# Sinkhorn attention and a four-expert layer: one score stage two slots forward, one weight load in two parts

## The chip, the cores and the metric

The kernel runs on one core of one Trainium2 chip. The metric is the device time of one execution in microseconds (us). Before the change it is 362.58 us (median of three runs, 362.51 to 362.75). The profile covers one further execution of 362.67 us, whose instructions span 360.9 us.

The engines carry the profile's names: PE is the matrix engine (TensorE), PEld its weight loads, DVE is VectorE, ACT is ScalarE, POOL is GpSimd, SP is SyncE. L414 is line 414 of the kernel before.

## The reference, cut to what matters

An attention over four batches of eight heads with 768 tokens, whose keys and values are mixed among eight blocks by a doubly normalized matrix, feeds a layer of four experts.

```python
def _attn_ref(q, k, v, sort_net):            # q, k, v: (4, 8, 768, 64), sort_net: (4, 8, 8, 8)
    P = sort_net
    for _ in range(5):                       # exp, rows to sum 1, columns to sum 1
        ...
    k_sorted = np.einsum('bhij,bhjcd->bhicd', P, k_b).reshape(B, H, S, D)
    v_sorted = np.einsum('bhij,bhjcd->bhicd', P, v_b).reshape(B, H, S, D)
    ...
    scores = scale * np.matmul(q_b, k_sb.transpose(0, 1, 2, 4, 3))   # within a block of 96 tokens
    attn = np.exp(scores - max) ; attn = attn / (sum + 1e-9)
    return np.matmul(attn, v_sb)

def _moe_ref(x, domain_probs, w1, w2):       # x: (3072, 512), w1: (4, 512, 1024), w2: (4, 1024, 512)
    p = domain_probs / (domain_probs.sum(-1, keepdims=True) + 1e-09)
    for e in range(E):
        h = np.maximum(x @ w1[e], 0.0)
        out += p[:, e:e + 1] * (h @ w2[e])
```

## The kernel before, where the change touches it

The instruction order of every engine is the order of the program text. The experts' layers of one batch run on PE while the attention of a later batch is done in small stages between them. A stage handles one pair of heads. These are the stages that matter here; `psa` hands out the tiles of one PSUM pool, `psm` those of another, and each pool has two buffers that are taken in turn.

```python
    psM = ... tc.tile_pool(name="psM", bufs=2, space=PSUM)     # hidden layers and outputs of the experts
    psA = ... tc.tile_pool(name="psA", bufs=2, space=PSUM)     # attention stages

    def st_k(b, pr):                  # mixed keys of a pair: 6 matmuls, four copies by ACT
        ps = psa([P, 2, 512], F32, f"ps_k_{b}_{pr}")
        ...
        kT = kTs[pr % 2][...]
        ... nc.scalar.copy(kT[...], pk[...])                   # line 404

    def st_s(b, pr):                  # scores of a pair: both buffers, 16 matmuls, two exponentials by ACT
        kT, qT = kTs[pr % 2], qTs[(b, pr)]
        pss = [psa([P, 2, 512], F32, f"ps_s_{b}_{pr}_{hh}") for hh in range(2)]
        for i in range(NB):
            for hh in range(2):
                nc.tensor.matmul(pss[hh][...], kT[...], qT[...], start=True, stop=True)   # line 414
        for hh in range(2):
            nc.scalar.activation(ETs[2 * (pr % 2) + hh][...], pss[hh][...], AF.Exp, ...)  # line 421

    def normalize(ps, xsl, hh):       # DVE
        ...
        nc.vector.reciprocal(rz[:], av[:, :, :, D:D + 1])                                 # line 430
        nc.vector.tensor_tensor(xsl[...], av[:, :, :, 0:D], rz[:].broadcast_to(...), ALU.mult)

    def st_a(b, pr):                  # output of a pair: a buffer for each head, normalized by DVE
        ...
        for hh in range(2):
            ps = psa([P, 2, 512], F32, f"ps_a_{b}_{pr}_{hh}")
            for i in range(NB):
                nc.tensor.matmul(ps[...], ET[...], vs[...], start=True, stop=True)        # line 449
            normalize(ps, xsl, hh)

    # st_v(b, pr): mixed values (2 matmuls, a copy by ACT, line 361);  st_q: transposes queries by a transfer
```

The hidden layers of the experts are computed in groups. After each group a slot is called, in which the stages planned for that slot are put into the program. `Hb` and `Sb` hold a hidden layer and its sums.

```python
    def chunk_first(b, c, es, first, slot, weights=None):
        for e in es:
            for g in range(2):
                ps = psm([P, 4, 2 * P], F32, f"ps_h_{b}_{c}_{e}_{g}")
                ... nc.tensor.matmul(ps[:, f, :], w1sb[e][...], xT[...], ...)   # 16 of them, line 780
                nc.vector.scalar_tensor_tensor(out=Hb[...], in0=ps[:], ...)     # line 786
                ... h_sums(e - 1, w)                                            # DVE, lines 750 and 752, after g = 1
                slot()

    PLANS = {   # (chunk, slot, stage, batch, pair)
        1: [
            (0, 0, st_k, 2, 1), (0, 0, st_bk, 2, 1), (0, 1, st_lk, 3, 0), (0, 1, st_n, 3, 1), (0, 2, st_q, 2, 3), (0, 3, st_a, 2, 0),
            (0, 3, st_n, 3, 2), (0, 4, st_s, 2, 1), (0, 5, st_x, 2, 0), (0, 5, st_k, 2, 2), (0, 5, st_v, 2, 2),
            ... (0, 6, st_v, 2, 3), ... (0, 7, st_s, 2, 2), ...
```

The second matrix of expert 0 is loaded by one transfer from POOL's queue. PE uses it in `second_layer0`, four of its eight parts first, then a slot, then the other four.

```python
    def load_w2(e):
        nc.gpsimd.dma_start(w2sb[e][:], moe_w2[e].rearrange("(fc p) d -> p fc d", p=P))

    def second_layer0(hf, slot):
        for t in range(R // 2):
            ...
            for fc in range(NFC):                                               # NFC is 8
                nc.tensor.matmul(ps, h0(fc)[...], w2sb[0][:, fc, :], ...)       # line 704
                if fc == KH - 1:                                                # KH is 4
                    slot()
            if col == 0:
                own_weights(po[:, 1, 0:R])
            ...
            slot()

    load_half_queries(1)
    load_w2(0)
    build_PI0(nc.gpsimd, 1, 0, H, Rs[:, 0:H, HB:NB])                            # POOL, line 323
```

Of the kernel before, what the change touches and what calls it, by code (L numbers as in the profile page):

```python
# [17 lines left out]
def kernel(  # L18
# [11 lines left out]
    nc = tc.nc  # L30
# [8 lines left out]
    P = 128  # L39
# [5 lines left out]
    NFC = FF // P  # L45
# [80 lines left out]
    w1sb, w2sb = [], []  # L126
# [8 lines left out]
                w1sb[e][:, ds(i * n, n)], moe_w1[e].rearrange("(kc p) f -> p kc f", p=P)[:, ds(i * n, n)]  # L135
            )

    def load_w2(e):
        nc.gpsimd.dma_start(w2sb[e][:], moe_w2[e].rearrange("(fc p) d -> p fc d", p=P))

    def load_half_queries(hf):
        for qd in range(2):
            nc.gpsimd.dma_start(
                q0[ds(64 * qd, 64), hf].rearrange("p h r d -> p h (r d)"), half_queries(qd, hf)
            )
# [176 lines left out]
    def build_PI0(eng, a, h0, hn, src):  # L322
        eng.tensor_tensor(
            PI0[a][:, ds(h0, hn)],
            maskk[:, 0:HB * CP].rearrange("p (o i c) -> p o i c", o=1, c=CP).broadcast_to([P, hn, HB, CP]),
            src.rearrange("p g (i o) -> p g i o", o=1).broadcast_to([P, hn, HB, CP]),
            ALU.mult,
        )
# [280 lines left out]
    def st_bk(b, qd):  # L609
# [16 lines left out]
            (2, 9, st_k, 2, 0), (2, 9, st_lv, 3, 0), (2, 9, st_n, 3, 0), (2, 11, st_s, 2, 0), (2, 12, st_q, 2, 2),  # L626
        ],
        1: [
            (0, 0, st_k, 2, 1), (0, 0, st_bk, 2, 1), (0, 1, st_lk, 3, 0), (0, 1, st_n, 3, 1), (0, 2, st_q, 2, 3), (0, 3, st_a, 2, 0),
            (0, 3, st_n, 3, 2), (0, 4, st_s, 2, 1), (0, 5, st_x, 2, 0), (0, 5, st_k, 2, 2), (0, 5, st_v, 2, 2),  # L630
            (0, 5, st_n, 3, 3), (0, 6, st_v, 2, 3), (0, 6, st_lv, 3, 1), (0, 7, st_s, 2, 2), (0, 8, st_k, 2, 3),
            (0, 8, st_bv, 3, 0), (0, 9, st_bk, 3, 0), (0, 9, st_lk, 3, 1), (0, 9, st_q, 3, 0), (0, 10, st_a, 2, 1),
            (0, 11, st_s, 2, 3), (0, 12, st_a, 2, 2), (0, 12, st_x, 2, 1), (0, 12, st_q, 3, 1), (0, 13, st_v, 3, 0),
# [691 lines left out]
    mixed("k", 0, mk0, 2, 2, act)  # L1325
    vec(Rs.rearrange("p g (a i) -> p a g i", a=2), Rv.rearrange("p a i g -> p a g i"))
    load_half_queries(1)
    load_w2(0)
    build_PI0(nc.gpsimd, 1, 0, H, Rs[:, 0:H, HB:NB])
    h_w(0, vec, 0, 2, tails[("v", 0, 0)])  # L1330
    mixed("v", 0, mv0, 2, 2, vec)
# [50 lines left out]
    def builds(b):  # L1382
        for n in range(2 * b, 2 * b + 2):
            build_PI(nc.gpsimd, n, "v")
            build_PI(nc.gpsimd, n, "k")

    load_w2(1)
    load_w2(2)
    load_w1(3)
    load_w2(3)  # L1390
# [99 lines left out]
```

The softmax here doesn't subtract the row's maximum and nothing guards it: scores larger than these inputs give would overflow.

## Time and profile before

| what | before |
|---|---|
| time, median of 3 | 362.58 us |
| span of the profiled execution | 360.9 us |
| PE busy | 352.6 us |
| PE's wait in the score stage of line 414 for DVE | 1.3 us, in 2 waits |
| PE's wait at line 704 for the load of a second matrix | 0.4 us, 1 wait |

In the profile, busy time is the time in which an engine ran instructions; an engine's wait is its idle time just before an instruction, put down to whatever released that instruction last. In a list in order of time the columns are start, duration, engine, line, operation, what is written and read, and the number of instructions drawn together; idle time and its releaser follow in brackets. `ps_s` is the score tile, `ps_a` the output tile of the attention, `ps_h` a hidden layer, `xsl` the normalized output, `w` a weight matrix.

### The profile page before, as it was taken

To read this page: it belongs to the slowest core of one execution; us is meant where nothing else is said; L and a number is where in the kernel's file an instruction comes from. 1 tells how busy PE (TensorE), PEld (TensorE's weight loads), DVE (VectorE), ACT (ScalarE), POOL (GpSimd) and SP (SyncE) were. 2 spreads that over 40 slices of the span, in tenths; PEclk is the share of its full clock that TensorE was granted. 3 is DMA by queue.
4 is the path that set the end of the run, shared out by engine and by line. 5 is a ranking of instruction groups with operands and counts; after the bars stand their busy time and mean duration, and the time that the engine had idled before them with its cause. 6 is when DMAs were issued, how large, how long until landed. Compare 5 with 4: busy or idle time off the path is not lost.

```text
span 360.9 us, 9496 instructions
## 1 busy us (share of the span) xinstructions
PE 352.6 (98%) x3949; PEld 306.6 (85%) x3949; DVE 275.2 (76%) x549; ACT 172.4 (48%) x306; POOL 133.2 (37%) x148
## 2 busy tenths in 40 slices
PE   8899999999999989999999999999999999999995
PEld 8785857888888968988889888888888888888895
DVE  5753897769798677868988988896678886588962
ACT  2664440442425254367947348831289611688210
POOL 8882010367022420000534518840058800288400
PEclk9999999999999999999999999999999999999999
DMA  7999999999999999935995330004300016100011
GB/s 100 207 206 231 213 210 198 210 180 189 190 178 158 192 107 158 180 69 69 176 187 101 54 124 0 2 0 107 101 30 2 3 39 137 61 0 2 2 73 46
DMA packets 72007, 40.52 MB, mean 112 GB/s; under 512 B 40598, under 2 KB 66716, under 8 KB 71964
## 3 DMA queue, kind: packets, MB, share of 16 engines
q0 software_dynamic: 36560, 19.93, 42.6%
q1 hardware_dynamic: 35260, 19.92, 28.1%
q8 instruction: 31, 0.51, 0.6%
q14 instruction: 12, 0.10, 0.1%
q10 hardware_dynamic: 144, 0.07, 0.1%
HBM read 42.13 MB, written 6.34 MB: 134 GB/s over the span
## 4 chain that ended last, share of the span: by engine, by line
PE 87%; DMA 5%; DVE 4%; issue 1%; ACT 1%; POOL 1%; DVEq 0%; ACTq 0%
PE ps_h L780 17%; PE ps_Q L1234 16%; PE ps_p L764 12%; PE ps_X L1104 10%; PE ps_Z L1104 6%; PE ps_Q L1104 6%; PE ps_Z L1234 6%; DMA w<-in_moe_w_dram 4%; PE ps_o L704 3%; PE ps_p L815 3%; PE ps_s L414 2%; PE ps_h L669 1%; PE ps_a L449 1%; PE ps_v L361 1%; PE ps_k L395 1%
## 5 line engine op out<-in xcount | busy, mean ns | idle before, releaser
L780 PE MATMUL ps_h<-xT,w 128*128 128x256 f16 x576 | 67.5, 273 | 0.0
L780 PEld LDWEIGHTS <-w 128*128 128x128 f16 x576 | 55.2, 98 | 7.3
L786 DVE SCALAR_TENSOR_TENSOR Hb<-ps_h,pb 128x1024 f16<-128x1024 f32 x34 | 41.5, 1223 | 18.3 <-PE ps_h L780 17.9
L1104 PEld LDWEIGHTS <-w 128*128 128x128 f16 x480 | 43.5, 98 | 4.9 <-issue 0.2
L1117 POOL TENSOR_TENSOR arena<-tmp,pb 128x512 f16<-128x512 f32 x12 | 15.2, 1276 | 65.1 <-PE ps_Z L1104 49.8
L1234 PEld LDWEIGHTS <-Hb 128*128 128x128 f16 x320 | 31.1, 98 | 3.6
L421 ACT ACTIVATE ET<-ps_s 96x768 f16<-96x768 f32 x24 | 18.0, 802 | 30.8 <-PE ps_s L414 30.6
L1234 PEld LDWEIGHTS <-Sb 128*128 128x128 f16 x304 | 28.0, 98 | 3.4 <-DVE Sb L750 0.3
L1116 ACT ACTIVATE tmp<-tmp 128x512 f32<-128x512 f32 x46 | 28.9, 632 | 4.2 <-DVE tmp L1154 4.2
L1104 PEld LDWEIGHTS <-arena 128*128 128x128 f16 x312 | 27.8, 98 | 2.8
L404 ACT CAST kT<-ps_k 64x384 f16<-64x384 f32 x48 | 22.7, 473 | 14.0 <-PE ps_k L395 13.0
L121 POOL DMA_DIRECT2D arena<-in_q_dram x24 | 19.9, 843 | 18.2 <-DMA q_ring<-arena 17.1
L1104 PE MATMUL ps_X<-ET,arena 128*128 128x256 f16 x168 | 25.2, 272 | 0.0
L764 PEld LDWEIGHTS <-Hb 128*128 128x128 f16 x232 | 21.9, 98 | 3.0
L1234 PE MATMUL ps_Q<-w,Hb 128*128 128x256 f16 x192 | 24.4, 273 | 0.0
L1110 DVE SCALAR_TENSOR_TENSOR Hb<-ps_X,pb 128x512 f16<-128x512 f32 x27 | 18.6, 691 | 7.4 <-PE ps_X L1104 7.3
L1124 ACT COPY ps_X<-ps_Z 128x512 f32<-128x512 f32 x27 | 15.4, 570 | 18.1 <-PE ps_Z L1104 18.1
L1104 PE MATMUL ps_Z<-xT,w 128*128 128x256 f16 (+1 forms) x176 | 22.5, 258 | 0.1
L750 DVE TENSOR_TENSOR Sb<-Hb 128x512 f16<-128x512 f16 x33 | 21.2, 661 | 0.0
L1131 ACT COPY tmp<-ps_X 128x512 f32<-128x512 f32 x26 | 15.2, 585 | 8.8 <-PE ps_X L1104 6.2
L1110 DVE SCALAR_TENSOR_TENSOR Hb<-ps_Z,pb 128x512 f16<-128x512 f32 x27 | 18.4, 682 | 1.3 <-PE ps_Z L1104 1.3
L1154 DVE TENSOR_TENSOR tmp<-ps_Q,tmp 128x512 f32<-128x512 f32 x26 | 17.7, 681 | 0.8 <-PE ps_Q L1104 0.8
(261 smaller groups left out, 742.4 us busy)
## 6 DMA issues: line engine op xcount, KB each, us to landing
w<-in_moe_w_dram POOLq DMA_DIRECT2D x7, 1024.0 KB, 27.7
pb<-p_dram SPq DMA_DIRECT2D x9, 512.0 KB, 6.1
arena<-in_k_dram POOLq DMA_DIRECT2D x8, 384.0 KB, 8.6
arena<-in_v_dram POOLq DMA_DIRECT2D x8, 384.0 KB, 7.7
vs<-arena SPq DMA_DIRECT2D x36, 66.0 KB, 5.1
arena<-in_q_dram POOLq DMA_DIRECT2D x24, 96.0 KB, 7.3
out_dram<-ob SPq DMA_DIRECT2D x9, 256.0 KB, 2.1
out_dram<-oa SPq DMA_DIRECT2D x8, 256.0 KB, 2.4
```

Source lines behind the costliest of these rows:

```text
L121: nc.gpsimd.dma_start(t[:, h // 2, :, h % 2, :], q[b, h].rearrange("(t p) d -> p t d", p=P))
L404: nc.scalar.copy(kT[ds(D * hh, D), r], pk[ds(D * r, D), hh].rearrange("p a (i c) -> p a i c", c=CP),)
L421: nc.scalar.activation(ETs[2 * (pr % 2) + hh][:, 0:S].rearrange("c (a x) -> c a x", a=2), pss[hh][0:BLK, :, 0:HS], AF.Exp, bias=0.0, scale ...
L750: tt(sm[0], blk(0, 1), blk(1, 1), ALU.add)
L764: nc.tensor.matmul(ps, lhs(e, f), Ts[e][rhs][:, f, :], start=(first and e == es[0] and f == 0), stop=(done and e == es[-1] and f == KH - 1 ...
L780: nc.tensor.matmul(ps[:, f, :], w1sb[e][:, kc, ds((4 * g + f) * P, P)], xT[:, kc, ds(2 * c * P, 2 * P)], start=(kc == 0), stop=(kc == NKC ...
L786: nc.vector.scalar_tensor_tensor(out=Hb[:, homes.get(e, e), ds(4 * g, 4), :], in0=ps[:], scalar=0.0, op0=ALU.max, in1=weights(e).broadcast ...
L1104: nc.tensor.matmul(dst[:, ds(f * cols, cols)], a[lhs][:, k, ds((f0 + f) * P, P)], t[rhs][:, k, :], start=(first and f == 0 and k == 0), st ...
L1110: nc.vector.scalar_tensor_tensor(out=home(i, j), in0=src.rearrange("p (f x) -> p f x", f=m), scalar=0.0, op0=ALU.max, in1=weight(j).broadc ...
L1116: nc.scalar.activation(src, src, AF.Relu, bias=0.0, scale=1.0)
L1154: tt(t12, Q, u2, ALU.add)
L1234: nc.tensor.matmul(ps, lhs(e, f), Ts[e][rhs][:, f, part], start=(first and e == 0 and f == 0), stop=(e == E - 1 and f == KH - 1), skip_gro ...
```

## The change

In the plan for batch 1, the score stage of batch 2's second pair moves from slot 4 to slot 2 of the first chunk. It then stands ahead of `st_a` of the first pair, in slot 3, where it stood behind it. It is meant to keep the scores from having to wait until DVE has emptied the two buffers that `st_a` fills. The second matrix of expert 0 is loaded in two halves of four parts each, so that the first matmuls that use it depend on the first half alone.

```diff
-    def load_w2(e):
-        nc.gpsimd.dma_start(w2sb[e][:], moe_w2[e].rearrange("(fc p) d -> p fc d", p=P))
+    def load_w2(e, parts=1):
+        n = NFC // parts
+        for i in range(parts):
+            nc.gpsimd.dma_start(
+                w2sb[e][:, ds(i * n, n)], moe_w2[e].rearrange("(fc p) d -> p fc d", p=P)[:, ds(i * n, n)]
+            )
@@ PLANS @@
-            (0, 0, st_k, 2, 1), (0, 0, st_bk, 2, 1), (0, 1, st_lk, 3, 0), (0, 1, st_n, 3, 1), (0, 2, st_q, 2, 3), (0, 3, st_a, 2, 0),
-            (0, 3, st_n, 3, 2), (0, 4, st_s, 2, 1), (0, 5, st_x, 2, 0), (0, 5, st_k, 2, 2), (0, 5, st_v, 2, 2),
+            (0, 0, st_k, 2, 1), (0, 0, st_bk, 2, 1), (0, 1, st_lk, 3, 0), (0, 1, st_n, 3, 1), (0, 2, st_q, 2, 3), (0, 2, st_s, 2, 1), (0, 3, st_a, 2, 0),
+            (0, 3, st_n, 3, 2), (0, 5, st_x, 2, 0), (0, 5, st_k, 2, 2), (0, 5, st_v, 2, 2),
@@ program @@
-    load_w2(0)
+    load_w2(0, 2)
```

## The prediction

> **What bounds the kernel now.** I read the page's shares first, then who waits for whom on TensorE, then the order of time around each of its waits.
>
> ```profile
> PE 352.6 (98%) x3949; PEld 306.6 (85%) x3949; DVE 275.2 (76%) x549; ACT 172.4 (48%) x306; POOL 133.2 (37%) x148
> ```
>
> TensorE (PE) is busy 98% of the span, so only time in which it stands still can be won by moving work about. The second view is the list of waits on PE, longest total first (columns: total us, times, longest):
>
> ```profile
> PE ps_s L414 <- DVE xsl L431: 1.3, 2, 0.7
> ...
> PE ps_o L704 <- DMA w<-in_moe_w_dram: 0.4, 1, 0.4
> ```
>
> The other waits of note stand in the first 15 us. The first line is the score stage `st_s` held up by VectorE's normalizing in `st_a`; the second is expert 0's second matrix arriving late. The change goes at exactly these two. PE's instructions in order of time around the first (start, duration, line, tile; in brackets the idle time before):
>
> ```profile
> 119.36 5.40 PE L780 MATMUL ps_h<-xT,w 128*128 128x256 f16 x48
> 124.60 0.65 PE L449 MATMUL ps_a<-vs,ET 96*128 96x65 f16 x16
> 125.08 1.91 PE L780 MATMUL ps_h<-xT,w 128*128 128x256 f16 x16
> 127.70 0.21 PE L414 MATMUL ps_s<-q_ring,kT 64*128 64x96 f16 x1 [0.71 <-DVE xsl L431]
> 128.54 0.51 PE L414 MATMUL ps_s<-q_ring,kT 64*128 64x96 f16 x15 [0.62 <-DVE xsl L431]
> 128.98 1.92 PE L780 MATMUL ps_h<-xT,w 128*128 128x256 f16 x16
> ```
>
> And VectorE (DVE) in the same stretch:
>
> ```profile
> 124.80 1.22 DVE L786 SCALAR_TENSOR_TENSOR Hb<-ps_h,pb 128x1024 f16<-128x1024 f32 x1 [0.52 <-PE ps_h L780]
> 125.94 0.41 DVE L750 TENSOR_TENSOR Sb<-Hb 128x512 f16<-128x512 f16 x1
> 126.39 0.42 DVE L752 TENSOR_TENSOR Sb<-Sb,Hb 128x512 f16<-128x512 f16 x1
> 126.73 0.20 DVE L430 RECIPROCAL rz<-ps_a 96x8 f32<-96x8 f32 x1
> 126.96 0.69 DVE L431 TENSOR_TENSOR xsl<-ps_a,rz 96x512 f16<-96x512 f32 x1
> 127.57 0.19 DVE L430 RECIPROCAL rz<-ps_a 96x8 f32<-96x8 f32 x1
> 127.79 0.69 DVE L431 TENSOR_TENSOR xsl<-ps_a,rz 96x512 f16<-96x512 f32 x1
> 128.40 1.21 DVE L786 SCALAR_TENSOR_TENSOR Hb<-ps_h,pb 128x1024 f16<-128x1024 f32 x1
> ```
>
> `st_a` fills both buffers of the attention pool (two buffers, taken in turn) at 124.60. They come free only when DVE, which has the long multiplication L786 and two sums ahead of it, has normalized each: at 127.65 and 128.48. `st_s` needs both and gets them one by one. It would have taken 0.45 us (another `st_s`: 135.51 to 135.96) and takes from 126.83, where the hidden-layer group ahead of it ends, to 128.98.
>
> The second place, first on PE, then on GpSimd (POOL), which issues the loads:
>
> ```profile
> 28.51 1.04 PE L704 MATMUL ps_o<-w,Hb 128*128 128x512 f16 x4 [0.39 <-DMA w<-in_moe_w_dram]
> ```
>
> ```profile
> 13.92 0.92 POOL L139 DMA_DIRECT2D w<-in_moe_w_dram  x1
> 15.05 1.05 POOL L323 TENSOR_TENSOR Sb<-maskk,Rs 128x512 f16<-128x512 f16 x1 [0.21 <-DVE Rs L1326]
> ...
> 40.47 0.74 POOL L110 DMA_DIRECT2D arena<-in_k_dram  x1 [4.57 <-DMA w<-in_moe_w_dram]
> 46.18 0.74 POOL L110 DMA_DIRECT2D arena<-in_v_dram  x1 [4.97 <-DMA w<-in_moe_w_dram]
> ```
>
> The whole matrix, issued at 13.92, lands at 28.46; PE waits 0.39 us for it. POOL's later waits end 5.71 us apart, each with one more whole matrix landed: the loads come in one behind the other, about 5.7 us each.
>
> **What the Trainium skill says.** "Perfetto Trace Analysis", section Identifying Performance Opportunities (Optimization Strategy): look for the gaps on the contended engine and for what blocks there; recurring bubbles can mean too little PSUM for the next tile. The trace agrees: this gap is two buffers not yet free. The same page, DMA Optimizations: splitting a transfer may let some of the work start sooner, if the DMA engines are generally idle. Here they are not (9 tenths busy in this stretch), so I expect only the first half to be earlier, not the whole. "DMA: Bandwidth & Descriptors", section Queues, rings and completion order: each DMA engine takes its descriptors in ring order. The loads landing one behind the other agree, so the first half should land first.
>
> **Part 1, the score stage.** Nothing is added or removed: 16 matmuls and two exponentials go two slots forward, ahead of `st_a`. The instruction order of DVE and ScalarE (ACT) stays the same; on PE alone the block moves. I walk the new order with the durations above; 16 L780 matmuls take 1.75 us.
> - `st_s` comes after the group that ends at 119.36 + 2 x 1.75 = 122.86. Its `kT` is copied by ACT from 119.61 to 121.57, which also frees the buffer; its queries' transpose was issued at 111.28 and such transfers landed 4.1 us later. No wait: 122.86 to 123.31.
> - ACT starts an exponential 0.61 us after the stage starts (115.51 to 116.12) and takes 1.50 for the two: 123.47 to 124.97. It is free then.
> - Next group: 123.31 to 125.06. `st_a`: 125.06 to 125.55. It needs the two score buffers: the first is free at about 124.3, the second at 124.97, needed at 125.3. No wait, with 0.3 us in hand.
> - Groups of expert 2: 125.55 to 127.30 and to 129.05. Nothing stands in the old place of `st_s`.
> - DVE's row is 0.45 us later: L786 at 125.25, then the same 3.60 us as before (124.80 to 128.40) up to the next L786, 128.85 to 130.06. The normalizing ends at 128.10 and 128.93, ahead of `st_k` at 129.05 and `st_v` at 129.38. No wait there.
> - Expert 3's first group could begin at 129.05 + 0.66 = 129.71, but its buffer in the other pool comes free when that L786 ends: 130.06, plus some 0.06 as in the old waits, 130.13. So about 0.4 us of the wait comes back elsewhere. Before, this group began at 131.40: gain 1.27 us.
> - Before, `st_v` of pair 3 then waited 0.20 us (group end 133.15, start 133.35) for ACT's four `kT` copies ending at 133.29. In the new order those run from 129.64 to 131.60 and `st_v` comes at 131.88: 0.20 more. At the next `st_s`, old start 135.51, the gain is 1.47 us.
>
> All of it lies on the path: from there on PE runs nearly without gaps, and what small gaps there are (the longest listed is under 0.4 us) hang on other engines that move along with it.
>
> **Part 2, the split load.** One more DMA. A half takes about half of 5.7 us, so the first lands near 25.6 (estimate from the 5.7 above), 2.5 us before its use at 28.12; PE loses its 0.39 us. The second lands at 28.46 or little after; with the 4 matmuls (0.97) and the transposes in between (0.49) it is needed at about 29.6, 1.1 us later. Cost: POOL issues twice, and an issue takes 0.7 us even for a half (two of 512 KB: 1.43), so `build_PI0` begins near 15.4 in place of 15.05; its product is first used by the mixing at 23.04, so this is hidden. POOL's later issues slip by at most a microsecond or two, behind transfers that are queued until 51 anyway. Gain 0.39 us.
>
> **Sum.** 362.58 - 1.47 - 0.39 = 360.72. I take off nothing else and give back 0.1 for small new waits: **360.8 us**.
>
> **Rivals.** (a) *Vector work takes over fully.* If the sums or L786 run later than I have them, expert 3's group waits longer than 0.4 us. DVE is 76% busy and it alone sets 130.13 in my walk, which speaks for this one; against it, its work is the same 3.60 us in the same order. A wait of 1 us would leave 361.3. (b) *The moved stage waits itself*, for queries or for ACT, or `st_a` for the second exponential. Slacks: 1.3 us for `kT`, more than 7 for the queries, 0.3 for ACT. The last is the thin one; at worst some 0.3 us, 361.0. (c) *The early gain is absorbed.* A small transpose at 30.95 uses expert weights from a transfer issued at 25.77, whose landing the profile doesn't give. PE shows no wait there, so it landed by 30.95; but the small one ahead of it on that queue took 6.1 us (issued at 19.68, followed up at 25.77), so it may have landed only just in time, and then 0.39 earlier is waited for again: 361.1. (d) *The extra transfer hurts*: the eight waits in rotation on POOL shift by one and hold later loads, or the halves land later. The load of `w1` of expert 2 landed at about 40.4 and is used at 42.42, so there is room for 2 us. If it went past: 363.
>
> **Range and chances.** (a) to (c) each cost a few tenths and may add up to about 1.1: 361.9 above. Below, if DVE's wait doesn't come (0.4) and a small gap later closes: 360.2. Two percent is 7.3 us, far more than all PE waits together; so faster by over 2% 0.01, within 2% 0.98, slower 0.01.
>
> **What would show it.** After the change PE's wait `ps_s` on `xsl` around 127 is gone; a wait of L780 on DVE's `Hb` of 0.3 to 0.5 us stands near 130; `ps_s` of pair 2 starts near 133.6 (135.51 less 1.47 less 0.39); the wait for `w` at 28.5 is gone; DVE's and ACT's busy times are unchanged. Wrong it would be if a longer wait stands at `st_a` or at expert 3's group, if PE waits at 30 or 42 for a transfer, or if the saving at 133 is gone again at the end.

## The result, and the profile after

The changed kernel takes 361.38 us (median of 6 runs, 360.71 to 361.85) where the kernel before takes 362.54 (6 runs beside it, 362.45 to 362.80). The ratio is 0.9965 with a 95% interval of 0.9952 to 0.9978: 1.2 us faster, within 0.8 to 1.7. The profiled execution took 361.54 us. Line numbers of the changed kernel are four higher.

Who waits for whom on PE, after the change (total us, times, longest), and one line of the same list for its weight loads:

```profile
PE ps_h L673 <- DMA w<-in_moe_w_dram: 0.6, 1, 0.6
PE ps_mv L495 <- ACT kT L506: 0.6, 1, 0.6
PE ps_h L784 <- DVE Hb L790: 0.3, 1, 0.3
```

```profile
PEld L495 <- DMA arena<-in_v_dram: 0.7, 1, 0.7
```

Both waits that the change was aimed at are gone: none of `ps_s` L418 for `xsl`, none at L708 for the second matrix. Three others stand there. The last was foreseen. The first two stand in no such list of the kernel before, and lie before 20 us. The weight-load line shows that the second of them, put down to ACT, is really a wait for the values of batch 0.

PE in order of time around the moved stage:

```profile
123.20 0.51 PE L418 MATMUL ps_s<-q_ring,kT 64*128 64x96 f16 x16
123.65 1.92 PE L784 MATMUL ps_h<-xT,w 128*128 128x256 f16 x16
125.41 0.65 PE L453 MATMUL ps_a<-vs,ET 96*128 96x65 f16 x16
125.89 3.66 PE L784 MATMUL ps_h<-xT,w 128*128 128x256 f16 x32
129.39 0.50 PE L399 MATMUL ps_k<-arena 128*128 128x128 f16 x6
129.73 0.49 PE L365 MATMUL ps_v<-arena 128*128 128x384 f16 x2
130.48 1.91 PE L784 MATMUL ps_h<-xT,w 128*128 128x256 f16 x16 [0.26 <-DVE Hb L790]
132.22 0.49 PE L365 MATMUL ps_v<-arena 128*128 128x384 f16 x2
132.55 1.91 PE L784 MATMUL ps_h<-xT,w 128*128 128x256 f16 x16
134.39 0.52 PE L418 MATMUL ps_s<-q_ring,kT 64*128 64x96 f16 x16
```

And DVE in the same stretch (the last line draws two multiplications together):

```profile
125.61 1.23 DVE L790 SCALAR_TENSOR_TENSOR Hb<-ps_h,pb 128x1024 f16<-128x1024 f32 x1 [1.07 <-PE ps_h L784]
...
127.77 0.69 DVE L435 TENSOR_TENSOR xsl<-ps_a,rz 96x512 f16<-96x512 f32 x1
128.38 0.19 DVE L434 RECIPROCAL rz<-ps_a 96x8 f32<-96x8 f32 x1
128.61 0.69 DVE L435 TENSOR_TENSOR xsl<-ps_a,rz 96x512 f16<-96x512 f32 x1
129.22 2.34 DVE L790 SCALAR_TENSOR_TENSOR Hb<-ps_h,pb 128x1024 f16<-128x1024 f32 x2
```

The scores run at 123.20 without a wait, the normalizing ends before `st_k` at 129.39, and what remains is 0.26 us at 130.48, where expert 3's group waits for the first of the two multiplications. In the kernel before, that group came here:

```profile
131.40 1.91 PE L780 MATMUL ps_h<-xT,w 128*128 128x256 f16 x16
```

The beginning of the same execution:

```profile
16.32 0.57 PE L495 MATMUL ps_mv<-Sb,arena 128*64 128x64 f16 x24 [0.55 <-ACT kT L506]
...
19.57 0.83 PE L673 MATMUL ps_h<-xT,w 128*128 128x192 f16 x8 [0.64 <-DMA w<-in_moe_w_dram]
...
28.27 0.56 PE L271 MATMUL ps_q<-ident,T 64*64 64x64 f16 x24
28.77 1.04 PE L708 MATMUL ps_o<-w,Hb 128*128 128x512 f16 x4
```

And two places of the kernel before, to compare:

```profile
18.57 0.82 PE L669 MATMUL ps_h<-xT,w 128*128 128x192 f16 x8
...
27.56 0.57 PE L267 MATMUL ps_q<-ident,T 64*64 64x64 f16 x24
28.51 1.04 PE L704 MATMUL ps_o<-w,Hb 128*128 128x512 f16 x4 [0.39 <-DMA w<-in_moe_w_dram]
```

L708 is reached at 28.77 with no wait, but the kernel before was there at 28.51 *after* its wait: 1.2 us of new waiting near 16 and 19 has cost more than what was saved since. PE is 1.00 us late at the first matrix (19.57 for 18.57), still 0.71 late at the 24 transposes of queries (`ps_q`) just ahead of L708 (28.27 for 27.56), and 0.26 late at L708. The first half of the first matrix was issued at 6.26 in both and took this long to land, before and after the change (size, then us):

```profile
w<-in_moe_w_dram POOLq DMA_DIRECT2D x1, 512.0 KB, 11.8
```

```profile
w<-in_moe_w_dram POOLq DMA_DIRECT2D x1, 512.0 KB, 13.3
```

To take the two parts of the change apart, two landmarks cut every execution in three: the first matmul of expert 1's first group (G, in `chunk_first(0, 0, [1, 2], ...)`) and the first matmul of the last stage, `ps_X<-w` near 187 (X). The split lies before G, the moved stage between G and X. All figures are starts in a profiled execution, in us.

```profile
37.71 1.91 PE L780 MATMUL ps_h<-xT,w 128*128 128x256 f16 x16
...
187.50 0.38 PE L1055 MATMUL ps_X<-w 128*128 128x512 f16 x1
```

```profile
37.97 1.91 PE L784 MATMUL ps_h<-xT,w 128*128 128x256 f16 x16
...
186.37 0.38 PE L1059 MATMUL ps_X<-w 128*128 128x512 f16 x1
```

The first pair is the kernel before, the second the changed one.

| kernel | G | X | G to X | X to end of span |
|---|---|---|---|---|
| before | 37.71 | 187.50 | 149.79 | 173.40 |
| changed | 37.97 | 186.37 | 148.40 | 173.43 |

The moved stage is worth 1.39 us and keeps it to the end; the beginning was 0.26 us *longer*. The sum is the 1.13 us between the two profiled executions (362.67 and 361.54).

### The profile page after: what moved, and what is told of

Same layout as the page of the kernel before. It is cut to its first block, busy times and chain, and to the rows that moved or that the text cites. A ratio compares the mean times of both kernels' runs of the same rounds, so it can differ in the third digit from the quotient of the medians.

```text
span 359.8 us, 9499 instructions
## 1 busy us (share of the span) xinstructions
PE 351.8 (98%) x3949; PEld 306.2 (85%) x3949; DVE 275.0 (76%) x549; ACT 172.6 (48%) x306; POOL 133.9 (37%) x149
## 4 chain that ended last, share of the span: by engine, by line
PE 89%; DMA 4%; DVE 3%; issue 1%; POOL 1%; ACT 1%; DVEq 0%; ACTq 0%; POOLq 0%
PE ps_h L784 17%; PE ps_Q L1238 16%; PE ps_p L768 12%; PE ps_X L1108 10%; PE ps_Z L1108 6%; PE ps_Q L1108 6%; PE ps_Z L1238 6%; DMA w<-in_moe_w_dram 4%; PE ps_h L673 3%; PE ps_o L708 3%; PE ps_p L819 3%; PE ps_s L418 2%; PE ps_a L453 1%; PE ps_k L399 1%; PE ps_v L365 1%
## 5 line engine op out<-in xcount | busy, mean ns | idle before, releaser
L1120 ACT ACTIVATE tmp<-tmp 128x512 f32<-128x512 f32 x46 | 28.8, 631 | 4.2 <-DVE tmp L1158 4.2
L1158 DVE TENSOR_TENSOR tmp<-ps_Q,tmp 128x512 f32<-128x512 f32 x26 | 17.7, 681 | 0.8 <-PE ps_Q L1108 0.8
```

Source lines behind the costliest of these rows:

```text
L1120: nc.scalar.activation(src, src, AF.Relu, bias=0.0, scale=1.0)
L1158: tt(t12, Q, u2, ALU.add)
```

## The experiments

Two theories on the early loads stood at the outset. **A**: the score stage is worth about 1.4 us, as walked through; the split is worth its 0.4 us only in executions in which PE comes to the second matrix before it has landed, since early waits for other loads, which vary from execution to execution, stand in for that wait. **C**: the extra transfer delays the loads ahead of it, every time. (B, in e1's expectation, is that both parts are worth less than worked out.) The kernels e1 to e4, e5 to e8 and e9 to e12 each ran on one chip beside the kernel before, whose median was 362.70, 362.56 and 362.56 us, with a spread of 2 us or more; so ratios to it are given with their 95% intervals, and the readings rest on the landmarks. The edits are shown against the changed kernel, from e5 to e8 against e3; e3 and e4 load the second matrix whole.

**e1: the score stage alone**

```diff
-    load_w2(0, 2)
+    load_w2(0)
```

> The score stage moved, the load whole as before. Theory A (the move is worth what the walk says, the split is worth nothing or less): 361.1 to 361.2 us, 1.4 us less than before, no wait for a second-matrix load or values beyond those of before except the 0.4 us at line 704/708, and a small spread between executions like that of before (about 0.35 us). Rival B (both parts are worth less than worked out): 361.6 or more. In the profile, a wait of the hidden-layer group on VectorE of about 0.3 us near 130.

361.24 us, ratio 0.9966 (0.9954 to 0.9979). G to X is 148.41 us, so the move alone does all that the changed kernel does there. The whole load is back, and yet the list of waits has nothing for it:

```profile
19.35 0.83 PE L673 MATMUL ps_h<-xT,w 128*128 128x192 f16 x8 [1.01 <-DMA w<-in_moe_w_dram]
...
28.24 0.57 PE L271 MATMUL ps_q<-ident,T 64*64 64x64 f16 x24
28.82 1.04 PE L708 MATMUL ps_o<-w,Hb 128*128 128x512 f16 x4
```

Up to 113 us this is the program before, and it shows the same early wait as the changed kernel, longer even (1.01 us), with no split in it. PE reaches L708 so late that the whole matrix lands just then (issued near 13.88, 14.9 us to landing: 28.8). Waits under 0.15 us are not listed; from the transposes to L708 it is 0.58 us here and 0.50 in the changed kernel, so 0.08 us may be such a wait. The expectation of a small spread was wrong: 360.59 to 362.04.

**e2: the split alone**

```diff
-            ... (0, 2, st_q, 2, 3), (0, 2, st_s, 2, 1), (0, 3, st_a, 2, 0),
-            (0, 3, st_n, 3, 2), (0, 5, st_x, 2, 0), ...
+            ... (0, 2, st_q, 2, 3), (0, 3, st_a, 2, 0),
+            (0, 3, st_n, 3, 2), (0, 4, st_s, 2, 1), (0, 5, st_x, 2, 0), ...
```

> The load split, the score stage where it was. The prediction's step: 362.15 us, 0.4 less. Theory A (the wait for the whole matrix had hidden how late or early the first loads land; without it PE follows them, execution by execution): median between 362.0 and 362.9, and a spread between executions of 0.8 us or more where before has 0.35. Rival C (issuing the second half delays the loads ahead of it every time): 362.7 to 363.0 with waits for values and for the first matrix between 15 and 20 us in every trace.

362.24 us, ratio 0.9989 (0.9974 to 1.0003): 0.4 us less at the middle, and no difference is not excluded. The spread, 1.07 us, says nothing for theory A, since the kernel before spread over 3.31 us beside it. G is at 37.23, G to X 149.78 as before. The first matrix was waited for 0.47 us near 19, less than in e1 without the split, which speaks against C's "every time".

**e3: the sums later.** Is the 0.26 us left at 130 really the buffer that the multiplication holds? Expert 0's two sums go behind that multiplication.

```diff
+                hold = (b, c, e) == (1, 0, 2) and g == 0
+                if hold:
+                    for w in (1, 2):
+                        h_sums(0, w)
-                if e > first and (g or not late):
+                if e > first and (g or not late) and (b, c, e) != (1, 0, 1):
```

> As the score stage moved alone, and expert 0's two sums on VectorE (0.8 us) go behind the next group's multiplication, so that its buffer comes free 0.8 us sooner. If the remaining wait of about 0.3 us near 130 is the buffer of that group: the wait is gone, 0.25 to 0.3 us less than the score stage alone, 360.85. If the wait only moves to a later group: the same as the score stage alone, within 0.1.

360.81 us, ratio 0.9953 (0.9941 to 0.9965). In its profile the group starts without a wait:

```profile
130.13 0.49 PE L365 MATMUL ps_v<-arena 128*128 128x384 f16 x2
130.45 1.91 PE L784 MATMUL ps_h<-xT,w 128*128 128x256 f16 x16
```

```profile
128.82 1.21 DVE L790 SCALAR_TENSOR_TENSOR Hb<-ps_h,pb 128x1024 f16<-128x1024 f32 x1
129.95 0.41 DVE L754 TENSOR_TENSOR Sb<-Hb 128x512 f16<-128x512 f16 x1
```

G to X is 148.17 us, 0.24 less than e1: the wait is that buffer, and it doesn't move on. (G stood at 38.37 in this execution, behind 1.0 us of idle PE near 14 and 21 for which the profile names nothing.)

**e4: the score stage just ahead of `st_a`, in the same slot**

```diff
-            ... (0, 2, st_s, 2, 1), (0, 3, st_a, 2, 0),
+            ... (0, 3, st_s, 2, 1), (0, 3, st_a, 2, 0),
```

> The score stage just ahead of the first pair's output stage, in the same slot, with no hidden-layer group between; load whole. If ScalarE's exponentials (1.5 us for two, 0.6 us after the stage starts) hold the buffers that the output stage needs: PE waits 1.4 us at the output stage, and 0.2 us is left of the gain: 362.3. If only the order of the two stages counted: 361.15 as with the two slots.

362.44 us, ratio 1.0000 (0.9986 to 1.0014). PE around the two stages:

```profile
124.94 0.51 PE L418 MATMUL ps_s<-q_ring,kT 64*128 64x96 f16 x16
126.41 0.40 PE L453 MATMUL ps_a<-vs,ET 96*128 96x65 f16 x8 [0.95 <-ACT ET L425]
127.11 0.40 PE L453 MATMUL ps_a<-vs,ET 96*128 96x65 f16 x8 [0.30 <-ACT ET L425]
```

Order alone is worth 0.16 us (G to X 149.63). The output stage now waits 1.25 us for ACT's exponentials. The group of hidden-layer matmuls between the two stages, 1.75 us, is what covers them.

**e5 to e8: two loads, each whole or in finer parts.** The base is e3. In e6 the second matrix comes in halves, in e7 expert 0's first matrix in four quarters of 256 KB in the order of use, in e8 both.

```diff
-    load_w1(0, 2)
+    def load_w1_quarter(i, j):
+        nc.gpsimd.dma_start(
+            w1sb[0][:, ds(2 * i, 2), ds(512 * j, 512)],
+            moe_w1[0].rearrange("(kc p) f -> p kc f", p=P)[:, ds(2 * i, 2), ds(512 * j, 512)],
+        )
+    for j in range(2):
+        load_w1_quarter(0, j)
...                                   (behind the memsets of the constants)
+    for j in range(2):
+        load_w1_quarter(1, j)
```

> The score stage moved and the sums later, all loads as before: the base of the three that follow, once more. 360.8 us; in the profile one early wait of PE, either for the first half of expert 0's first matrix near 19 or for its second matrix near 28, not both in full.

> The base with the second matrix in halves. Theory (the wait near 28 is paid only in executions whose first matrix came early; where it came late, PE has lost that time already): between 0 and 0.3 us less than the base. The prediction's step: 0.4 less. Rival (the extra transfer hurts): 0.2 or more above the base.

> The base with expert 0's first matrix in four quarters, in the order of use, the second matrix whole. Theory: the wait near 19 goes, but PE then meets the wait near 28 in full (0.4 to 1 us), so 0 to 0.4 us less than the base. Rival (only the first matrix counts): 0.6 to 0.9 less.

> Both loads in parts on the base. Theory (the two waits stand in for each other, so both have to go): 0.6 to 1.0 us less than the base, more than the other two together, near 360.0. Rival (they add up): the sum of the other two. If the early loads merely land when they land and other values are waited for: no less than the better of the two.

| kernel | time, range | ratio, interval | G | G to X | waits of PE before G, other than those of every run |
|---|---|---|---|---|---|
| e5, base | 361.01, 360.43 to 361.67 | 0.9950, 0.9933 to 0.9967 | 37.93 | 148.19 | 0.70 for values, 0.15 for the second matrix |
| e6, second matrix in halves | 360.90, 360.32 to 361.41 | 0.9949, 0.9932 to 0.9965 | 37.17 | 148.18 | 0.40 for the first matrix |
| e7, first matrix in quarters | 361.04, 360.96 to 361.19 | 0.9954, 0.9938 to 0.9971 | 37.53 | 148.18 | 0.47 for the second matrix |
| e8, both | 360.55, 360.31 to 363.19 | 0.9948, 0.9934 to 0.9962 | 37.17 | 148.18 | 0.19 for values |

The 0.15 of e5 is not in the list of PE's waits; the transposes are 0.65 us ahead of L708 there, for 0.50 in e6, and the list of weight loads has 0.2 us for the second matrix. The wait for values is not one of the two that e5's expectation names.

e7 is the telling one. With the first matrix in time, PE meets the wait for the second again:

```profile
28.34 1.04 PE L718 MATMUL ps_o<-w,Hb 128*128 128x512 f16 x4 [0.47 <-DMA w<-in_moe_w_dram]
```

Its five times have the smallest spread of all, 0.23 us. In e8 that wait is gone. By medians, e7 takes 0.03 us more than the base, e6 0.11 less and e8 0.46 less: e8 gains more than the two apart, as its expectation has it, but under the 0.6 expected, and inside the intervals. Nor does G of e8 lie earlier than G of e6 (37.17 both). That both loads have to be split is so made likely by e7's wait, and is not shown by the times. e8 has the lowest median of all kernels here, 0.5% under the kernel before.

**e9 and e10: the first matrix surely late.** 384 KB of queries go ahead of it.

```diff
+    load_half_queries(1)
     load_w1(0, 2)
...
-    load_half_queries(1)
     load_w2(0)            # e9; e10: load_w2(0, 2)
```

> The score stage moved, the second matrix whole; the second half of batch 0's queries (384 KB) is loaded ahead of expert 0's first matrix, not behind it, so that this matrix lands some 2 us later while the second matrix lands where it did. Theory (the two early waits stand in for each other): PE waits 1.5 to 3 us near 20 and then none at all near 28; 1.3 to 2.5 us above the score stage alone.

> The same with the second matrix in halves. Theory: with the first matrix surely late the split is worth nothing, within 0.2 us of the same kernel with the load whole. The prediction's step (0.4 us whatever the rest): 0.4 less.

e9 took 363.19 us, ratio 1.0022 (1.0008 to 1.0036), e10 363.10, ratio 1.0015 (1.0002 to 1.0028). Two executions of e9 over 367 us, one of them its only profile, are left out, and so is the beginning of e11's profile below: the clock granted to PE was lowered there (0.99 over the span). That the order of the early loads costs some 2 us is seen: e12 and e11, with the order as it was, took 360.91 and 361.09. Whether the split is worth nothing here is not. The medians differ by 0.09, which fits the theory, but each kernel spreads over 3 us. e10's trace fits it too: 1.34 us of waiting for the first matrix at 19.84, none near 28; it is of e10's fastest execution (361.99), and shows what is waited for, not how long as a rule.

**e11 and e12: the changed kernel and the score stage alone, on one chip**, unedited.

> The changed kernel, beside the score stage alone on one chip. The prediction's step: 0.4 us less than the score stage alone. Theory: 0 to 0.4 less, 0.2 in the middle, by execution; in the trace a wait for the first matrix or the values before 20 us, none near 28.

> The score stage alone, for comparison with the changed kernel: 361.1 to 361.3 us; from the first group of expert 1 (near 38) to the first matmul of the last stage (near 186) 148.4 us as before in this kernel, whatever the early waits do.

e11 took 361.09 us, ratio 0.9964 (0.9954 to 0.9975), e12 360.91, 0.2 below its expectation, ratio 0.9961 (0.9950 to 0.9973). With the split no gain is seen: the median is 0.18 us higher. G to X is 148.41 and 148.42. In e12's profile hardly anything was late: G at 37.15, the earliest of every run, with the load whole. It landed 14.0 us after its issue near 13.9, and PE comes shortly before, 0.16 us by the distance of the transposes (0.66 for 0.50):

```profile
27.30 0.56 PE L271 MATMUL ps_q<-ident,T 64*64 64x64 f16 x24
27.96 1.04 PE L708 MATMUL ps_o<-w,Hb 128*128 128x512 f16 x4
```

## Why the prediction was right, and where it was off

The time lies inside the range, and the direction and most of the size are right; of 1.86 us worked out, 1.16 were measured. The range, 360.2 to 361.9, also had room for the split to bring nothing; so the time alone does not show that both terms were right, and one was not.

- **The score stage.** Worked out 1.47 us, measured 1.39 (G to X, before and changed). Both parts of it came as described: at expert 3's group the gain is 1.18 us counted from G (131.40 - 37.71 less 130.48 - 37.97) in place of 1.27 (the walk is 0.08 us early from its first step: the scores start at 122.94, with the 0.26 of G taken off, for 122.86), and another 0.20 at `st_v`, whose 0.20 us gap is closed. e1 shows that the move alone does it.
- **Vector work partly in its place** (the walk's 0.4 us, rival a). There, as 0.26 us at the expected instruction. The DVE row between the two multiplications was 3.61 us, against the 3.60 carried over. e3 shows that it is the buffer and that it can be had.
- **ACT's exponentials, 0.3 us in hand** (rival b). No wait in the changed kernel; e4 takes the cover away and they cost 1.25 us.
- **The split's 0.39 us: the term that was mis-sized.** The step "PE loses its 0.39 us" took the wait of one profiled execution as a fixed cost. The first half did land earlier, 12.4 us after its issue at 13.88, so at 26.3 where 25.6 was estimated, the second behind it, at about 28.8, and the wait at L708 did go. (The Trainium skill, "Perfetto Trace Analysis", DMA Optimizations, names idle DMA engines for the whole task to end sooner, not, as the prediction has it, for some of the work to start sooner; here the first half landed sooner with these engines 9 tenths busy.) But what that is worth hangs on what came before. The first half of the *first* matrix is issued alike in all kernels of this list, near 6.26, and lands at different times. With the second matrix whole that took 11.8 us (before), 13.0 (e1), 12.3 (e3), 13.1 (e4), 12.8 (e5) and 11.4 (e12), with it in halves 13.3, 12.5 (e2) and 12.5 (e6): from 17.7 to 19.6. PE wants it near 18.5. Where it is late, PE comes late to the second matrix too, and the whole of that has all but landed (e1); where it is early, the second is waited for (before, e7 with its first matrix in quarters, and a little in e12).

  The distance from the transposes to L708 gives the size, with waits too short for the list. With the load in halves it is 0.50 us in the changed kernel, e2 and e6. With it whole it is 0.95 in the kernel before, 0.58 in e1, 0.50 in e3, 0.55 in e4, 0.65 in e5 and 0.66 in e12, six profiles of one and the same program up to G. So the whole load held PE for 0 to 0.45 us, 0.15 in the mean of the six, and the profile that the prediction read was the dearest of them.

  In the changed kernel's profiled execution the early waits took 1.2 us and the term came out as -0.26. Theory C, that the split itself delays the loads ahead, finds no support, since the landings with and without it overlap; three profiles with it are too few to exclude a small delay. By medians the split was worth 0.46 us (e2 to before), -0.18 (e11 to e12) and 0.11 (e6 to e5), each with an interval of some 0.5 us each way against the kernel before alone, which agrees with some 0.15 and does not settle it.
- **The early gain absorbed** (rival c). The idea was right and the transfer wrong: not the small one at 30.95 behind it, but the larger ones ahead of it.
- **The extra transfer hurting later loads** (rival d). Two issues took 1.53 us and `build_PI0` began at 15.40, both about as worked out. Later issues slipped further than thought (the builds at 25.24, from 22.71), and PE has no load after 28 in its list of waits.

What makes the early loads land up to 1.9 us apart stays open. They share 16 DMA engines that are 9 tenths busy there, but no run took any of that load away.

## What to carry to other kernels

When a stage that fills all buffers of a pool stands behind one whose buffers a busy engine frees, put it ahead, with enough matmuls between the two to cover its own evacuation: order alone brought 0.16 us here, order and 1.75 us of cover 1.39. A wait for one of several loads in a row, seen in a single profile, is not its price: ask what the engine would have waited for just before it, and look at a second execution. Splitting a load helped here only where its consumer was on time; the loads ahead of it in the queue may have to be split first (e7).

## What the runs showed of the hardware

Between the two landmarks the time of one and the same stretch of program repeats to 0.05 us over executions and chips (148.40 to 148.45 in the five profiles that share it), while its beginning does not: in the six profiles with the same program up to G, G lies between 37.15 and 38.37 us. A matmul that waits for a PSUM buffer starts 0.05 us after the instruction that frees it ends (DVE ends at 127.65, PE starts at 127.70 in the kernel before). To issue a load of 512 KB costs POOL about 0.76 us, twice in 1.53 in the changed kernel.
